# Windowed attention with a rational feed-forward network: transposes of q, k and P issued singly between the products of the network

## The chip, the core and the metric

The kernel runs on one core of a Trainium2 chip. A core has a matrix engine (TensorE, PE in the profile; its weight loads are shown apart as PEld), VectorE (DVE), ScalarE (ACT), GpSimd (POOL) and SyncE (SP), which here only issues DMAs. Each engine works through its own instructions in their order and waits on semaphores for the others. The metric is the device time of one execution in microseconds (us).

## The reference

Attention over a window, then a feed-forward network (FFN) whose activation is a ratio of polynomials. Cut to what matters:

```python
scores = q @ k.T / 8 + bias          # q, k, v: batch 4, heads 8, sequence 768, 64 each
scores = where(keep, scores, -1e9)   # keep: the last 96 keys, or one of the first 8
a = exp(scores - max); a = a / a.sum()
x = (a @ v) as [3072 tokens, 512]
h = x @ w_in                         # 512 -> 2048
P = a0 + a1*h + a2*h**2 + a3*h**3
Q = 1 + |b0|*|h| + |b1|*h**2
out = (P / (Q + 1e-6)) @ w_out       # 2048 -> 512
```

## The kernel before, in words

The 3072 tokens are cut into 12 chunks of 256 (TOK). A chunk has 8 attention units (two blocks of 128 queries, four pairs of heads) and 8 FFN units (two of the 16 tiles of 128 hidden features each). So there are 96 attention units u and 96 FFN units f. The function windowed() runs a pipeline over steps t: step t holds the splitting and transposing of q and k of unit t, the scores and the softmax of unit t-2, the transposing of its probabilities P for unit t-3, the product with v for two units at every odd step (st_pv), the first FFN product of f = t-12 (LAG) and the second of f-2 (F2).

Numbers are float32 held as a high and a low part in the type float32r, so each FFN product is taken three times (high by high, low by high, high by low). A step has on PE:

- st_ffn1: 24 products into a tile h, with 256 columns each (L258);
- st_ffn2: 12 products into two accumulators acc, with 512 columns each (L334); of each three, the third reads the low part of g, which POOL writes last (L314);
- st_score: 4 products into s (L408);
- st_qkT: 4 transposes of 128 x 128 into a tile tk (L378), from a tile sp that DVE and POOL write (L369, L370);
- st_pT: 4 transposes of P into a tile tp (L462), 2 in the first block of a sequence. From unit 30 (RAW) on P comes as float32r in the tile raw, which a DMA fills (L452) and which has one buffer; before unit 30 the transposes are plain float32;
- st_pv, at odd steps: 8 or 16 products into o, 64 output partitions each (L480).

The tiles tk, tp, s and o share three buffers in PSUM (pool ps_t). ACT copies tk out (L392, L395). DVE copies tp out (L465) from unit 21 (EARLY) on.

The order on each engine isn't that of the source. Each part gets a priority (base + 1000 t + a number from the table PRI), and the framework's scheduler walks a modelled timeline and issues, on each engine, what is ready by the model with the lowest priority first. That order is fixed when the program is built. In PRI, ffn1a is 150, qkT 200, pv 250, ffn1b 550, ffn2a 750, pT 800 and ffn2b 850: the four transposes of q and k stand between the two halves of st_ffn1, those of P between the two halves of st_ffn2, where they are ready by then.

Of the kernel before, what the change touches and what calls it, by code (L numbers as in the profile page):

```python
# [26 lines left out]
F2 = 2  # L27
# [68 lines left out]
def tile_kernel(ctx: ExitStack, tc: tile.TileContext, q, k, v, n_global, n_local,  # L96
# [11 lines left out]
    FPC = NFT // 2  # L108
    assert UPC == FPC == 8 and D == 64 and NT % 2 == 0
    NU = NCH * UPC  # L110
# [10 lines left out]
    def unit(u):  # L121
        c, j = divmod(u, UPC)
        t, p = divmod(j, NPAIR)
        b, i = divmod(2 * c + t, NT)
        return c, t, p, b, i

    def st_load(u):
        c, t, p, b, i = unit(u)
        hs = slice(2 * p, 2 * p + 4)
        r = slice(i * P, (i + 1) * P)  # L130
        n = pl.ldp.tile([P, 2, 4, D], F32, tag="nat", name=f"nat{u}")
        nc.sync.dma_start(out=n[:, 0], in_=q[b, hs, r, :].rearrange("h s d -> s h d"))
        nc.sync.dma_start(out=n[:, 1], in_=k[b, hs, r, :].rearrange("h s d -> s h d"))
        vt = pl.ldp.tile([P, 4, D], F32, tag="vt", name=f"vt{u}", bufs=6)
        nc.sync.dma_start(out=vt, in_=v[b, hs, r, :].rearrange("h s d -> s h d"))
        nat[u // 2] = n
        vts[u // 2] = vt
# [12 lines left out]
    def w_hi(key):  # L150
        if key[0]:
            return win_h[:, key[1], key[2] * 2 * TOK:(key[2] + 1) * 2 * TOK]
        return wout_h[:, key[1], :]

    def tmp(name):
        return pl.ffn.tile([P, 2, TOK], F32, tag="tmp", name=name, bufs=pl.tmps)
# [65 lines left out]
    a0, a1, a2, a3, b0, _, b1, q1 = (coef[:, x:x + 1] for x in range(8))  # L222
# [16 lines left out]
        nc.vector.tensor_scalar(out=k, in0=m, scalar1=0.0, scalar2=0.5, op0=ALU.is_gt, op1=ALU.mult)  # L239
        nc.vector.tensor_tensor(out=b1, in0=z, in1=k, op=ALU.mult)  # L240

    def st_ffn1(f, y):
        c, j = divmod(f, FPC)
        if y == 0:
            hps[f] = pl.ps_h.tile(sh, F32, tag="h", name=f"h{f}")
        jw, fw = divmod((2 * j + y) * P, 2 * TOK)
        fs = slice(fw, fw + P)
        if c == 0 and not pl.split:
            for ct in range(NCT):
                nc.tensor.matmul(out=hps[f][:, y, :], lhsT=full[1, ct, jw][:, fs], rhs=xT[c][:, ct, :],  # L250
                                 start=(ct == 0), stop=(ct == NCT - 1))
            return
        xh, xl = xT[c]
        n = 0
        for ct in range(NCT):
            wh, wl = w_hi((1, ct, jw)), low[1, ct, jw]
            for w, x in ((wh, xh), (wh, xl), (wl, xh)):
                nc.tensor.matmul(out=hps[f][:, y, :], lhsT=w[:, fs], rhs=x[:, ct, :],  # L258
                                 start=(n == 0), stop=(n == 3 * NCT - 1))
                n += 1  # L260

# [2 lines left out]
    def is_last(f):  # L266
        return f == NU - 1 and not pl.split
# [48 lines left out]
    def last_half(f, y):  # L316
        for st in (st_ew1, st_ew2, st_ew3, st_ew4):
            st(f, slice(y, y + 1))

    def st_ffn2(f, t):  # L320
        c, j = divmod(f, FPC)
        if j == 0:
            accs[c, t] = pl.ps_o.tile([P, DM], F32, tag="acc", name=f"acc{c}_{t}")
        acc = accs[c, t]
        ts = slice(t * P, (t + 1) * P)
        for y in range(2):
            ft = 2 * j + y
            if c == 0 and not pl.split:
                nc.tensor.matmul(out=acc, lhsT=gs[f][:, y, ts], rhs=full[0, ft],
                                 start=(ft == 0), stop=(ft == NFT - 1))  # L330
                continue
            wh = w_hi((0, ft))
            for n, (z, w) in enumerate(((0, wh), (0, low[0, ft]), (1, wh))):
                nc.tensor.matmul(out=acc, lhsT=gs[f][:, z, y, ts], rhs=w,  # L334
                                 start=(ft == 0 and n == 0), stop=(ft == NFT - 1 and n == 2))
        if j == FPC - 1:
            o = tmp(f"o{c}_{t}").rearrange("p a b -> p (a b)")
            rows = slice(c * TOK + t * P, c * TOK + (t + 1) * P)
            if is_last(f):
                (nc.vector.tensor_copy if t else nc.scalar.copy)(out=o, in_=acc)  # L340
            else:
                nc.any.tensor_copy(out=o, in_=acc)
            nc.sync.dma_start(out=out[rows, :], in_=o)
# [26 lines left out]
        nc.gpsimd.tensor_tensor(out=s[:, :, :, 1, :], in0=n, in1=s[:, :, :, 0, :], op=ALU.subtract)  # L370
        sp[u] = s

    def st_qkT(u):
        s = sp.pop(u)
        tk = pl.ps_t.tile([P, 2, 2, P], FR, tag="t", name=f"tk{u}")
        for z in range(2):
            for x in range(2):
                nc.tensor.transpose(out=tk[:, z, x, :], in_=s[:, z, x].rearrange("p a d -> p (a d)"),  # L378
                                    identity=ident_r)
        tqk[u] = tk  # L380


# [69 lines left out]
        nc.sync.dma_start(out=blocks_of(raw.bitcast(F32), i), in_=blocks_of(pr, i))  # L452
        prob[u] = (raw, None)

    def st_pT(u):
        i = unit(u)[4]
        pr, st = prob.pop(u)
        W = 2 if i else 1
        t_ps = pl.ps_t.tile([P, 2, 2, P], FR if u >= RAW else F32, tag="t", name=f"tp{u}")
        for x in range(2):  # L460
            for w in range(W):
                nc.tensor.transpose(out=t_ps[:, x, w, :], in_=pr[:, x, w, :], identity=ident_r if u >= RAW else ident)  # L462
        pT = pl.att.tile([P, 2, 2, P], F32, tag="pT", name=f"pT{u}", bufs=2)
        t_ps = t_ps.bitcast(F32) if u >= RAW else t_ps
        (nc.scalar.copy if u < EARLY else nc.vector.tensor_copy)(out=pT[:, :, 0:W, :], in_=t_ps[:, :, 0:W, :])  # L465
        pTs[u] = pT
# [33 lines left out]
        nc.vector.tensor_tensor(out=xl[:, p:p + 2, cs], in0=o_ps, in1=xh[:, p:p + 2, cs], op=ALU.subtract)  # L500


    ni = const.tile([P, 4], I32, name="ni")
    nf = const.tile([P, 4], F32, name="nf")

    def windowed():
        st_load(0)
        st_load(2)
        nc.sync.dma_start(out=ni[:, 0:2], in_=n_local.bitcast(I32).partition_broadcast(P))
        nc.sync.dma_start(out=ni[:, 2:4], in_=n_global.bitcast(I32).partition_broadcast(P))  # L510
        make_identity(nc, ident)
        nc.vector.tensor_copy(out=ident_r, in_=ident)
        nc.vector.tensor_copy(out=nf, in_=ni)
        load_coef()
        st_split(0)
        st_split(1)

        nl, ng = nf[:, 0:1], nf[:, 2:3]
        scr = tmp("scr").rearrange("p a (b w) -> p (a b) w", w=P)
        scr = [scr[:, x, :] for x in range(4)]  # L520
        window_masks(nc, scr, mask0, masks, nl, ng)

        base = tc.cur_priority
        for t in range(NU + LAG + F2):
            f = t - LAG
            pri = PRI_A if f < FPC else PRI

            def on(name, fn, u, *args):
                if 0 <= u < NU:
                    tc.cur_priority = base + 1000 * t + pri[name]  # L530
                    fn(u, *args)

            if t % 2 == 0:
                on("load", st_load, t + 4)
            on("score", st_score, t - 2)
            on("soft", st_soft, t - 2)
            on("ffn1a", st_ffn1, f, 0)
            on("qkT", st_qkT, t)
            if t % 2:
                on("pv", lambda u: st_pv(u // 2), t - 5)  # L540
            on("qkE", st_qkE, t)
            if t % 2:
                on("x", lambda u: st_x(u // 2), t - 5)
            if t:
                on("split", st_split, t + 1)
            if not is_last(f - 1):
                on("ew3", st_ew3, f - 1)
            on("norm", st_norm, t - 2)
            on("raw", st_raw, t - 2)
            if is_last(f):  # L550
                st_ew4(f - 1)
                last_half(f, 0)
                st_ffn1(f, 1)
                last_half(f, 1)
            else:
                on("ffn1b", st_ffn1, f, 1)
                on("ew1", st_ew1, f)
                if not is_last(f - 1):
                    on("ew4", st_ew4, f - 1)
                on("ew2", st_ew2, f)  # L560
            on("ffn2a", st_ffn2, f - F2, 0)
            on("pT", st_pT, t - 3)
            on("ffn2b", st_ffn2, f - F2, 1)
            for n, (kind, j) in enumerate(WSCHED.get(t, ())):
                tc.cur_priority = base + 1000 * t + pri["dec"] + 50 * n
                (load_win if kind else load_wout)(j)
            for n, key in enumerate(list(full)[SPLITS.get(f - 1, 0):SPLITS.get(f, 0)]):
                tc.cur_priority = base + 1000 * t + pri["wsplit"] + 4 * n
                split_w(key)
        tc.cur_priority = base + 1000 * (NU + LAG + F2 + 4)  # L570
# [154 lines left out]
```

## Time and profile before

| | |
|---|---|
| time, median of 3 runs | 794.26 us (793.93 to 798.46) |
| profiled execution: its time, its span | 792.2 us, 790.4 us |
| busy: PE, PEld | 743.9 us (94%), 649.6 us (82%) |
| busy: DVE, ACT, POOL | 599.6 us (76%), 575.1 us (73%), 533.3 us (67%) |
| granted clock of PE, mean | 0.992 |

A row of a timeline reads: start, duration, engine, line, operation, output and inputs, shape, count of instructions in the row, and in brackets the idle time before it and what ended it. Matmuls are pipelined, so a row's duration holds the time through the array as well; what one instruction costs in a stream is the distance from its start to the start of the next. The starts are printed in hundredths of a microsecond.

### The profile page before, as it was taken

To read this page: it belongs to the slowest core of one execution; us is meant where nothing else is said; L and a number is where in the kernel's file an instruction comes from. 1 tells how busy PE (TensorE), PEld (TensorE's weight loads), DVE (VectorE), ACT (ScalarE), POOL (GpSimd) and SP (SyncE) were. 2 spreads that over 40 slices of the span, in tenths; PEclk is the share of its full clock that TensorE was granted. 3 is DMA by queue.
4 is the path that set the end of the run, shared out by engine and by line. 5 is a ranking of instruction groups with operands and counts; after the bars stand their busy time and mean duration, and the time that the engine had idled before them with its cause. 6 is when DMAs were issued, how large, how long until landed. Compare 5 with 4: busy or idle time off the path is not lost.

```text
span 790.4 us, 15799 instructions
## 1 busy us (share of the span) xinstructions
PE 743.9 (94%) x5184; PEld 649.6 (82%) x5184; DVE 599.6 (76%) x1453; ACT 575.1 (73%) x1407; POOL 533.3 (67%) x572
## 2 busy tenths in 40 slices
PE   3688978899999999999999999999999999999995
PEld 2467647688998899999899999989999999988993
DVE  5889999987778676777776786777677786776664
ACT  4778677667887777777777777777877777766763
POOL 3868558979877667666667667666677777664440
PEclk9999999899999999999999999999999999999999
DMA  7785445212222233333332332333332332210000
GB/s 183 212 240 173 114 125 189 49 48 54 55 81 68 85 92 87 97 88 86 82 87 82 106 84 81 106 84 82 88 85 77 101 92 78 82 55 14 28 1 32
DMA packets 111932, 72.19 MB, mean 91 GB/s; under 512 B 82912, under 2 KB 97248, under 8 KB 111840
## 3 DMA queue, kind: packets, MB, share of 16 engines
q1 hardware_dynamic: 111840, 71.08, 32.0%
q8 instruction: 44, 0.72, 0.4%
q14 instruction: 48, 0.39, 0.2%
HBM read 35.92 MB, written 6.29 MB: 53 GB/s over the span
## 4 chain that ended last, share of the span: by engine, by line
PE 81%; DVE 6%; POOL 5%; DMA 4%; issue 2%; ACT 1%; SPq 0%; DVEq 0%; POOLq 0%; ACTq 0%
PE h L258 32%; PE acc L334 31%; PE o L480 5%; PE s L408 5%; PE tp L462 3%; PE tk L378 3%; DMA r<-in_moe_w_in_dram 2%; POOL pr L441 2%; PE h L250 1%; POOL sp L370 1%; DMA nat<-in_k_dram 1%; POOL fa L291 1%; DVE pr L419 1%; DVE fu L305 0%; DMA r<-in_moe_w_out_dram 0%
## 5 line engine op out<-in xcount | busy, mean ns | idle before, releaser
L334 PE MATMUL acc<-wout_h,g 128*128 128x512 f32 x704 | 242.8, 403 | 0.8 <-ACT g L313 0.8
L258 PE MATMUL h<-xh,win_h 128*128 128x256 f32 x704 | 205.4, 292 | 1.8 <-DVE fu L290 1.8
L441 POOL TENSOR_SCALAR pr<-pr,stats 128x256 f32<-128x256 f32 (+1 forms) x192 | 178.5, 940 | 39.2 <-issue 12.7
L258 PE MATMUL h<-xl,win_h 128*128 128x256 f32 x704 | 198.7, 282 | 0.0
L291 POOL TENSOR_TENSOR fa<-fa,fs 128x512 f32<-128x512 f32 x95 | 125.1, 1317 | 100.7 <-ACT fs L284 97.4
L334 PEld LDWEIGHTS acc<-wout_h,g 128*128 128x128 f32 x704 | 126.6, 188 | 21.8 <-ACT g L313 1.2
L258 PEld LDWEIGHTS h<-xh,win_h 128*128 128x128 f32 x704 | 133.3, 189 | 10.9 <-issue 6.2
L258 PEld LDWEIGHTS h<-xl,win_h 128*128 128x128 f32 x704 | 133.3, 189 | 2.3 <-issue 0.2
L429 ACT ACTIVATE pr<-pr,stats 128x256 f32<-128x256 f32 (+1 forms) x192 | 93.5, 492 | 53.5 <-DVE stats L419 53.4
L370 POOL TENSOR_TENSOR sp<-nat,sp 128x256 fp32r<-128x256 f32 x96 | 75.8, 790 | 73.5 <-DVE stats L432 41.0
L314 POOL TENSOR_TENSOR g<-fu,g 128x512 fp32r<-128x512 f32 x87 | 112.7, 1295 | 7.7 <-DVE fu L290 4.6
L282 ACT ACTIVATE fu<-h,coef 128x512 f32<-128x512 f32 (+1 forms) x97 | 75.4, 778 | 54.1 <-PE h L258 49.6
L303 DVE SCALAR_TENSOR_TENSOR fu<-fu,coef,q 128x512 f32<-128x512 f32 (+1 forms) x97 | 71.6, 738 | 36.2 <-ACT q L299 35.0
L298 ACT ACTIVATE fs<-fa,coef 128x512 f32<-128x512 f32 (+1 forms) x97 | 70.2, 724 | 30.3 <-POOL fa L291 27.9
L289 DVE TENSOR_TENSOR fu<-fu,h 128x512 f32<-128x512 f32 (+1 forms) x97 | 65.6, 677 | 16.9 <-ACT fs L284 14.9
L465 DVE COPY pT<-tp 128x512 f32<-128x512 f32 (+1 forms) x75 | 48.5, 646 | 35.7 <-PE tp L462 35.0
L369 DVE CAST sp<-nat 128x256 fp32r<-128x256 f32 x96 | 38.3, 399 | 46.7 <-PE tk L378 15.1
L290 DVE SCALAR_TENSOR_TENSOR fu<-fu,coef,h 128x512 f32<-128x512 f32 (+1 forms) x97 | 71.7, 739 | 2.5
L419 DVE CUSTOM_DVE_ANT_0 pr<-s,masks 128x256 f32<-128x256 f32 x160 | 61.4, 420 | 15.2 <-PE s L408 13.3
L408 PE MATMUL s<-kT,qT 128*128 128x256 f32 x384 | 70.5, 305 | 1.8 <-DMA qT<-qT 1.7
L304 DVE SCALAR_TENSOR_TENSOR q<-fa,coef,q 128x512 f32<-128x512 f32 (+1 forms) x97 | 72.1, 744 | 0.0
L408 PEld LDWEIGHTS s<-kT,qT 128*128 128x128 f32 x384 | 61.5, 203 | 9.0 <-DMA qT<-qT 1.9
(273 smaller groups left out, 1658.8 us busy)
## 6 DMA issues: line engine op xcount, KB each, us to landing
raw<-pr SPq DMA_DIRECT2D x58, 256.0 KB
qT<-qT SPq DMA_DIRECT2D x192, 64.0 KB
r<-in_moe_w_in_dram SPq DMA_DIRECT2D x16, 512.0 KB
r<-in_moe_w_out_dram SPq DMA_DIRECT2D x16, 512.0 KB
nat<-in_q_dram SPq DMA_DIRECT2D x48, 128.0 KB
nat<-in_k_dram SPq DMA_DIRECT2D x48, 128.0 KB
vt<-in_v_dram SPq DMA_DIRECT2D x48, 128.0 KB
out_dram<-o SPq DMA_DIRECT2D x24, 256.0 KB
```

Of the source, the lines that this page charges most:

```text
L258: nc.tensor.matmul(out=hps[f][:, y, :], lhsT=w[:, fs], rhs=x[:, ct, :], start=(n == 0), stop=(n == 3 * NCT - 1))
L282: nc.scalar.activation(out=u, in_=h, func=AF.Identity, scale=a3, bias=a2)
L290: nc.vector.scalar_tensor_tensor(out=u, in0=u, scalar=a1, in1=h, op0=ALU.add, op1=ALU.mult)
L291: side(f).tensor_tensor(out=a, in0=a, in1=s, op=ALU.add)
L303: nc.vector.scalar_tensor_tensor(out=u, in0=u, scalar=a0, in1=r, op0=ALU.add, op1=ALU.mult)
L304: nc.vector.scalar_tensor_tensor(out=r, in0=a, scalar=q1, in1=r, op0=ALU.add, op1=ALU.mult)
L314: side(f).tensor_tensor(out=g[:, 1, ys], in0=u, in1=g[:, 0, ys], op=ALU.subtract)
L334: nc.tensor.matmul(out=acc, lhsT=gs[f][:, z, y, ts], rhs=w, start=(ft == 0 and n == 0), stop=(ft == NFT - 1 and n == 2))
L370: nc.gpsimd.tensor_tensor(out=s[:, :, :, 1, :], in0=n, in1=s[:, :, :, 0, :], op=ALU.subtract)
L408: nc.tensor.matmul(out=s_ps[:, x], lhsT=qT[:, z, x, :], rhs=rhs, start=(z == 0), stop=(z == 1))
L429: nc.scalar.activation(out=d, in_=d, func=AF.Exp, scale=-1.0, bias=st[:, x:x + 1], accum_out=st[:, 2 + 2 * x:3 + 2 * x])
L441: nc.gpsimd.tensor_scalar(out=d, in0=d, scalar1=st[:, 6 + x:7 + x], scalar2=None, op0=ALU.mult)
```

## The change

st_ffn1, st_ffn2, st_qkT and st_pT become generators that pause after each instruction on PE. A new function weave runs two of them together: after every second product of the FFN it takes one transpose, with priorities that rise by 4 per product, so that the transposes have their places among the products of st_ffn1(f, 0) (12 products, q and k) and of both halves of st_ffn2 (12 products, P). It is used at steps 20 to 95 (FPC <= f < NU - 1 and t < NU); the other steps use the whole generators as before. What is computed is the same, and so is the number of instructions of each kind.

```diff
-    def st_ffn1(f, y):
+    def gen_ffn1(f, y):
...
                 nc.tensor.matmul(out=hps[f][:, y, :], lhsT=w[:, fs], rhs=x[:, ct, :],
                                  start=(n == 0), stop=(n == 3 * NCT - 1))
                 n += 1
+                yield
...
-    def st_ffn2(f, t):
+    def gen_ffn2(f, t):
...
                 nc.tensor.matmul(out=acc, lhsT=gs[f][:, z, y, ts], rhs=w,
                                  start=(ft == 0 and n == 0), stop=(ft == NFT - 1 and n == 2))
+                yield
...
-    def st_qkT(u):
+    def gen_qkT(u):
...
                 nc.tensor.transpose(out=tk[:, z, x, :], in_=s[:, z, x].rearrange("p a d -> p (a d)"),
                                     identity=ident_r)
+                yield
...
-    def st_pT(u):
+    def gen_pT(u):
...
                 nc.tensor.transpose(out=t_ps[:, x, w, :], in_=pr[:, x, w, :], identity=ident_r if u >= RAW else ident)
+                yield
...
+    def whole(gen):
+        def part(*args):
+            for _ in gen(*args):
+                pass
+        return part
+
+    st_ffn1, st_ffn2, st_qkT, st_pT = map(whole, (gen_ffn1, gen_ffn2, gen_qkT, gen_pT))
+
+    def weave(pri, main, other, every):
+
+        n = 0
+        for n, _ in enumerate(main):
+            if n % every == every - 1:
+                tc.cur_priority = pri + 4 * n + 2
+                next(other, None)
+            tc.cur_priority = pri + 4 * n + 4
+        for _ in other:
+            pass
...
-            on("ffn1a", st_ffn1, f, 0)
-            on("qkT", st_qkT, t)
+            woven = FPC <= f < NU - 1 and t < NU
+            if woven:
+                tc.cur_priority = base + 1000 * t + pri["ffn1a"]
+                weave(tc.cur_priority, gen_ffn1(f, 0), gen_qkT(t), 2)
+            else:
+                on("ffn1a", st_ffn1, f, 0)
+                on("qkT", st_qkT, t)
...
-            on("ffn2a", st_ffn2, f - F2, 0)
-            on("pT", st_pT, t - 3)
-            on("ffn2b", st_ffn2, f - F2, 1)
+            if woven and f - F2 >= 0:
+                tc.cur_priority = base + 1000 * t + pri["ffn2a"]
+                weave(tc.cur_priority, (x for y in range(2) for x in gen_ffn2(f - F2, y)), gen_pT(t - 3), 2)
+            else:
+                on("ffn2a", st_ffn2, f - F2, 0)
+                on("pT", st_pT, t - 3)
+                on("ffn2b", st_ffn2, f - F2, 1)
```

The order on PE around one group of transposes of q and k, before, at a step with products into o (a row ends with its count where it holds several instructions):

```order
L258 MATMUL h_8485<-xl_7291,win_h 128x256
L258 MATMUL h_8485<-xh_7290,w_3_2l 128x256
L378 MATMUL tk_8498<-ident_r,sp_8416 128x128 x4
L480 MATMUL o_8503<-pT_8366,vt_7555 64x128 x2
L480 MATMUL o_8503<-pT_8366,vt_7157 64x128 x2
L480 MATMUL o_8503<-pT_8464,vt_7555 64x128 x2
L480 MATMUL o_8503<-pT_8464,vt_7157 64x128 x2
L258 MATMUL h_8485<-xh_7290,win_h 128x256
```

The same step on PE now, at the transposes:

```order
L258 MATMUL h_8485<-xh_7290,win_h 128x256
L258 MATMUL h_8485<-xl_7291,win_h 128x256
L380 MATMUL tk_8488<-ident_r,sp_8416 128x128
L258 MATMUL h_8485<-xh_7290,w_0_2l 128x256
L258 MATMUL h_8485<-xh_7290,win_h 128x256
L380 MATMUL tk_8488<-ident_r,sp_8416 128x128
L258 MATMUL h_8485<-xl_7291,win_h 128x256
L258 MATMUL h_8485<-xh_7290,w_1_2l 128x256
L380 MATMUL tk_8488<-ident_r,sp_8416 128x128
L258 MATMUL h_8485<-xh_7290,win_h 128x256
L258 MATMUL h_8485<-xl_7291,win_h 128x256
L380 MATMUL tk_8488<-ident_r,sp_8416 128x128
```

And a little later in that step on PE, at the products into o:

```order
L258 MATMUL h_8485<-xl_7291,win_h 128x256
L258 MATMUL h_8485<-xh_7290,w_0_2l 128x256
L484 MATMUL o_8503<-pT_8370,vt_7555 64x128 x2
L484 MATMUL o_8503<-pT_8370,vt_7157 64x128 x2
L484 MATMUL o_8503<-pT_8468,vt_7555 64x128 x2
L484 MATMUL o_8503<-pT_8468,vt_7157 64x128 x2
L258 MATMUL h_8485<-xh_7290,win_h 128x256
```

One run of four has become four single transposes, each behind two products of the FFN, and the products into o, which followed the last transpose, now follow a product into h.

The transposes of P on PE, before:

```order
L334 MATMUL acc_0_8248<-wout_h,g_8349 128x512
L334 MATMUL acc_0_8248<-w_4l,g_8349 128x512
L334 MATMUL acc_1_8262<-wout_h,g_8349 128x512
L334 MATMUL acc_1_8262<-w_4l,g_8349 128x512
L258 MATMUL h_8485<-xh_7290,win_h 128x256
L258 MATMUL h_8485<-xl_7291,win_h 128x256
L258 MATMUL h_8485<-xh_7290,w_0_2l 128x256
L462 MATMUL tp_8459<-ident_r,raw_8326 128x128 x4
L334 MATMUL acc_0_8248<-wout_h,g_8349 128x512 x2
```

The same on PE now:

```order
L335 MATMUL acc_0_8248<-wout_h,g_8349 128x512
L335 MATMUL acc_0_8248<-w_4l,g_8349 128x512
L465 MATMUL tp_8455<-ident_r,raw_8326 128x128
L335 MATMUL acc_0_8248<-wout_h,g_8349 128x512 x2
L465 MATMUL tp_8455<-ident_r,raw_8326 128x128
L335 MATMUL acc_0_8248<-w_5l,g_8349 128x512
L335 MATMUL acc_0_8248<-wout_h,g_8349 128x512
L465 MATMUL tp_8455<-ident_r,raw_8326 128x128
L335 MATMUL acc_1_8262<-wout_h,g_8349 128x512
L335 MATMUL acc_1_8262<-w_4l,g_8349 128x512
L465 MATMUL tp_8455<-ident_r,raw_8326 128x128
```

Here too the run of four is taken apart, and the third product of an accumulator, the one that reads the low part of g, stands behind two products and one transpose, where four products, three of the next h and the transposes stood ahead of it.

## The prediction

> **What bounds the kernel now.** I read the page first: which engine is full, and what the chain of waits is made of.
>
> ```profile
> PE 743.9 (94%) x5184; PEld 649.6 (82%) x5184; DVE 599.6 (76%) x1453; ACT 575.1 (73%) x1407; POOL 533.3 (67%) x572
> PEclk9999999899999999999999999999999999999999
> PE 81%; DVE 6%; POOL 5%; DMA 4%; issue 2%; ACT 1%; SPq 0%; DVEq 0%; POOLq 0%; ACTq 0%
> ```
>
> PE carries 81% of the chain at a clock near full speed. An average over stages hides where it is full, so I cut the span into stretches with the view of windows (first column the length, then busy time and count by engine).
>
> ```profile
> 131.00:160.00 29.00, 25.23 (x143) 19.29 (x142) 28.26 (x63) 20.52 (x50) 27.10 (x24) 0.88 0.32 90
> 160.00:260.00 100.00, 100.00 (x722) 88.57 (x721) 79.31 (x181) 75.33 (x186) 79.30 (x83) 1.00 0.24 62
> 260.00:700.00 440.00, 440.00 (x3303) 398.66 (x3302) 322.88 (x807) 333.93 (x832) 307.27 (x341) 1.00 0.31 88
> 700.00:722.00 22.00, 22.00 (x158) 19.78 (x157) 16.88 (x36) 15.41 (x30) 11.26 (x10) 1.00 0.11 38
> ```
>
> From 160 to 722 us PE has no gap, while DVE has 440 - 322.9 = 117 us free in the long stretch, ACT 106 and POOL 133. Busy is not yet full, since a PE row also holds the time through the array, so I looked at whether starts follow each other at the pace of the work itself. The timeline of PE around one run of four transposes:
>
> ```profile
> 409.46 0.28 PE L258 MATMUL h<-xh,w_2l 128*128 128x256 f32 x1
> 409.58 0.46 PE L378 MATMUL tk<-ident_r,sp 128*128 128x128 f32 x4
> 409.87 0.35 PE L258 MATMUL h<-xh,win_h 128*128 128x256 f32 x1
> 410.06 0.28 PE L258 MATMUL h<-xl,win_h 128*128 128x256 f32 x1
> 410.18 0.29 PE L258 MATMUL h<-xh,w_2l 128*128 128x256 f32 x1
> 424.39 0.46 PE L378 MATMUL tk<-ident_r,sp 128*128 128x128 f32 x4
> ```
>
> A product into h starts 0.12 us after the one before it (410.06 to 410.18). The transposes of the next step but one begin at 424.39, 14.81 us on: a step takes 7.4 us. Its 24 products into h (2.8 us), 12 into acc (12 x 0.235 = 2.8, from the rows below) and 4 into s at the price of those into h (0.5), two groups of transposes (0.7) and half of a group into o make that up. So the pace is PE's own work, in order, and whatever the change adds to that work between 160 and 722 us is added to the time. All steps whose transposes are taken apart lie there.
>
> **What a transpose costs, alone and in a run.** The run of four at 409.58 delays the stream as follows: from its first start to the start of the second product behind it are 0.48 us, of which one product is 0.12, so four cost 0.36. The second product is the one to look at, since the first shows its start early and stays longer (0.35 instead of 0.28). The trace of before also has transposes of P in runs of one and three:
>
> ```profile
> 257.77 0.40 PE L334 MATMUL acc<-wout_h,g 128*128 128x512 f32 x1
> 258.01 0.40 PE L334 MATMUL acc<-w_10l,g 128*128 128x512 f32 x1
> 258.24 0.22 PE L462 MATMUL tp<-ident_r,raw 128*128 128x128 f32 x1
> 258.58 0.39 PE L334 MATMUL acc<-wout_h,g 128*128 128x512 f32 x1
> 259.27 0.37 PE L462 MATMUL tp<-ident_r,raw 128*128 128x128 f32 x3
> 259.48 0.46 PE L334 MATMUL acc<-wout_h,g 128*128 128x512 f32 x1
> 259.78 0.39 PE L334 MATMUL acc<-w_10l,g 128*128 128x512 f32 x1
> 265.07 0.22 PE L462 MATMUL tp<-ident_r,raw 128*128 128x128 f32 x1
> 265.42 0.39 PE L334 MATMUL acc<-wout_h,g 128*128 128x512 f32 x1
> 279.98 0.23 PE L462 MATMUL tp<-ident_r,raw 128*128 128x128 f32 x1
> 280.32 0.39 PE L334 MATMUL acc<-wout_h,g 128*128 128x512 f32 x1
> ```
>
> A product into acc takes 0.235 us (257.77, 258.01, 258.24). The three singles take 0.34, 0.35 and 0.34 to the second product behind them, less 0.235: 0.11 us each. The three in a run take 0.51 - 0.235 = 0.28. With 0.36 for four the costs are 0.11, 0.28, 0.36: about 0.084 for each transpose, and 0.027 more for each run, however long. Four singles cost 0.44 where a run costs 0.36.
>
> Why, the weight loads show:
>
> ```profile
> 258.01 0.14 PEld L462 LDWEIGHTS tp<-ident_r,raw 128*128 128x128 f32 x1
> 258.25 0.30 PEld L334 LDWEIGHTS acc<-wout_h,g 128*128 128x128 f32 x2
> 258.59 0.19 PEld L334 LDWEIGHTS acc<-w_11l,g 128*128 128x128 f32 x1
> ```
>
> The transpose's load, begun at 258.01, is hidden under the product before it. The product's load begins only with the transpose (258.25), and of the two merged loads the second begins at 258.25 + 0.30 - 0.19 = 258.36, 0.11 later: a product's load needs 0.11 us, and a single transpose, which streams 0.06 (its first in a run of four is followed that fast), can't cover it. In a run the next load is a transpose's, which is shorter. So a single hides one load and lays bare a longer one, four times over instead of once.
>
> The Trainium skill (TensorE: Matmul & The Clock Gate, section "LDWEIGHTS (loading the stationary operand)") prices any load at its columns over 1.2 GHz, an estimate of 107 ns for 128 columns. The single agrees; the run of four, at 0.36 and not 0.43, doesn't, and by that rule the taking apart would cost nothing and the whole change 2.0 us.
>
> **The change part by part.**
>
> 1. *Runs.* Counted in the order of the built programs, the float32r transposes (384 of q and k, 248 of P from unit 30 on) stand in 95 + 79 = 174 runs before and in 235 + 207 = 442 now; 369 of the runs now are single. Not every group is taken apart: at 19 steps those of q and k stand as three and one, at the early steps often still as four. 268 more runs x 0.027 = +7.2 us. Each of these numbers has an edge: at 0.020 for a run (singles of 0.105) it is 5.4, at 0.032 it is 8.6. No row shows a single between products into h; its load has the same 128 columns and type as that of acc, so I take the same price.
> 2. *Transposes of P in plain float32* (before unit 30): 46 runs before, 47 now. Nothing.
> 3. *What follows the transposes.* At odd steps the products into o stood behind the run and now stand behind a product into h. Both cases are in the trace:
>
> ```profile
> 253.51 0.28 PE L258 MATMUL h<-xh,w_3l 128*128 128x256 f32 x1
> 253.63 0.28 PE L258 MATMUL h<-xh,win_h 128*128 128x256 f32 x1
> 253.84 0.66 PE L480 MATMUL o<-pT,vt 128*64 128x128 f32 x8
> 402.04 0.46 PE L378 MATMUL tk<-ident_r,sp 128*128 128x128 f32 x4
> 402.42 0.66 PE L480 MATMUL o<-pT,vt 128*64 128x128 f32 x8
> ```
>
> A product into h ahead of o takes 0.21 instead of 0.12, 0.09 lost; a run of four ahead of o takes 0.38 instead of 0.36, 0.02 lost. The order has 41 such places behind transposes before and 12 now, 6 behind h before and 35 now: 29 x 0.07 = +2.0 us (between 0, if the o behind h hide it elsewhere, and 2.6).
>
> 4. *Moved earlier.* The first transpose of q and k comes up to ten products, 1.2 us, sooner. Its operand is long there, as in the step shown above:
>
> ```profile
> 403.06 0.74 POOL L370 TENSOR_TENSOR sp<-nat,sp 128x256 fp32r<-128x256 f32 x1
> ```
>
> It ends at 403.80, 5.8 us ahead of 409.58: free. The transposes of P read raw, whose DMA waits for the last transpose of the unit before, as there is one buffer:
>
> ```profile
> 378.50 0.64 SPq L452 DMA_DIRECT2D raw<-pr  x1
> 383.55 0.29 PE L462 MATMUL tp<-ident_r,raw 128*128 128x128 f32 x2
> ```
>
> Here 5.05 us from issue to use suffice without a gap on PE. Now the last of P stands 6 products and 3 transposes behind the first, 6 x 0.235 + 3 x 0.11 = 1.74 us, so 7.4 - 1.7 = 5.7 us remain from the last to the next unit's first, less the few tenths to the issue. Enough, as far as these rows tell. Behind the DMA on SP's queue stand the loads of later units and the moves of qT; they are used a step or more later.
> 5. *Moved later.* DVE's copy of P (L465) now waits for a last transpose that is 1.5 us further from the first than in a run (1.74 against 0.21). On DVE's queue behind it stand the next polynomial step (L290) and the reading of the scores; DVE's 117 us free over 440 / 7.4 = 60 steps are 1.96 us a step, so 1.5 fit. What is late next is g:
>
> ```profile
> 483.20 1.29 POOL L314 TENSOR_TENSOR g<-fu,g 128x512 fp32r<-128x512 f32 x1
> 485.54 0.40 PE L334 MATMUL acc<-wout_h,g 128*128 128x512 f32 x1
> ```
>
> The tightest step I found has 485.54 - 484.49 = 1.05 us between g and the first product into acc, and the third product, the first that reads that part, now comes 2 x 0.235 + 0.11 = 0.58 later: 1.6 us of cover against 1.5 of delay. I cost it at nothing.
>
> Sum: 7.2 + 2.0 = +9.2 us. The profiled execution (792.2, its span 790.4 and 1.8 around it) would take 801.4; the median of the runs, 794.26, lies 2.1 higher, so 803.5.
>
> **The rivals.**
>
> *Faster: the loads are hidden.* If PE fetched the load behind a single early, under the product ahead, a single would cost only its 0.06 us. Per row: 369 singles x 0.06 = 22.1, the other 263 transposes in 73 runs 263 x 0.084 + 73 x 0.027 = 24.1, together 46.2, against 632 x 0.084 + 174 x 0.027 = 57.8 before: -11.6, with the 2.0 of o -9.6, and 784.7 us. It decides at a single of about 0.086. For it speaks that loads do run under products; against it, that all three singles shown take 0.11. The Trainium skill (same page, section "Part 2: What happens when you issue a matmul") says that PE pulls loads ahead of running matmuls into a background buffer. The trace agrees for one load ahead and shows none for two. Chance 0.07.
>
> *No change that can be measured.* If a transpose costs the same in a run as alone (0.11 by the load behind it, which is what the skill's rule on loads above comes to), or the added pace is given back where other engines were late, only the o remain: about 796.3. For it speaks that the run's advantage rests on differences of hundredths; against it, that runs of one, three and four fit one line, and that PE has no gap to give back in. Chance 0.13.
>
> *Slower still: g or the copy of P becomes late.* The mechanism of 5: where the copy's delay exceeds the 1.6 us of cover, PE stands in order at the third product. Each 0.1 us beyond it, over the 63 steps with raw, is 6.3 us: 809.8 for 0.1. Against it speak the waits of DVE, 28.2 us in that stretch for P already, which PE never feels. Chance 0.10.
>
> ```profile
> DVE pT L465 <- PE tp L462: 28.2, 36, 1.7
> ```
>
> **How the numbers follow.** What this kernel's measurement can tell from no change is about 1%, 8 us: below 786.3 is faster, above 802.2 slower. The forecast (0.70) is 803.5, with 5.4 + 0 and 8.6 + 2.6 as the bounds of its terms 799.7 to 805.5; a quarter of it, 0.18, falls below 802.2. Faster 0.07; same 0.13 + 0.18 = 0.31; slower 0.52 + 0.10 = 0.62. The range goes from 796, the second rival, to 810, the third, and leaves out the first and parts of these two.
>
> **What would show it.** In the profile after: PE still without a gap from 160 to 722 us and the stretch some 9 us longer; singles at 0.11 between products into h too; steps of 7.5 instead of 7.4 us; no wait of PE for POOL's g or for raw. Singles at 0.06 would prove the first rival, unchanged steps the second; a wait of PE for g or for raw, or a stretch ahead of 160 us of another length, would make the number wrong for a reason that isn't in the sum.

## The result, and the profile after

The change takes 803.1 us in the median of its runs (798.74 to 805.61), the kernel before 794.1 us: a ratio of 1.0112, with a 95% interval of 1.0088 to 1.0136. Slower, by 9.0 us: little, but clear of the noise. The profiled execution is the lowest of the six, 798.74 us with a span of 796.9; experiments 7 and 9 to 11 look at why the totals differ.

The windows of the kernel after, with the same columns as before:

```profile
131.00:160.00 29.00, 26.52 (x167) 20.41 (x166) 27.98 (x63) 21.84 (x54) 27.10 (x25) 0.93 0.29 77
160.00:260.00 100.00, 99.42 (x716) 88.48 (x715) 82.71 (x187) 75.73 (x189) 79.28 (x83) 1.00 0.25 64
260.00:700.00 440.00, 440.00 (x3232) 391.10 (x3231) 309.33 (x787) 328.18 (x815) 298.82 (x335) 1.00 0.30 86
```

PE is still without a gap in the long stretch, but where 3303 of its instructions began there, 3232 do now: 2% fewer. Almost nothing new holds it up, since its waits from 160 to 715 us are one row, a single wait that lies ahead of 260 us:

```profile
PE h L258 <- DVE fu L291: 0.6, 1, 0.6
```

So the time went into the stream itself. The timeline of PE at transposes of q and k that stand singly, and, behind the dots, at products into o:

```profile
274.02 0.28 PE L258 MATMUL h<-xl,win_h 128*128 128x256 f32 x1
274.13 0.22 PE L380 MATMUL tk<-ident_r,sp 128*128 128x128 f32 x1
274.19 0.33 PE L258 MATMUL h<-xh,w_1l 128*128 128x256 f32 x1
274.36 0.28 PE L258 MATMUL h<-xh,win_h 128*128 128x256 f32 x1
274.48 0.23 PE L380 MATMUL tk<-ident_r,sp 128*128 128x128 f32 x1
274.55 0.33 PE L258 MATMUL h<-xl,win_h 128*128 128x256 f32 x1
274.71 0.28 PE L258 MATMUL h<-xh,w_1l 128*128 128x256 f32 x1
274.83 0.22 PE L380 MATMUL tk<-ident_r,sp 128*128 128x128 f32 x1
275.07 0.28 PE L258 MATMUL h<-xl,win_h 128*128 128x256 f32 x1
...
282.60 0.28 PE L258 MATMUL h<-xh,w_1l 128*128 128x256 f32 x1
282.81 0.77 PE L484 MATMUL o<-pT,vt 128*64 128x128 f32 x10
```

Each single takes 0.23 or 0.24 us to the second product behind it (274.13 to 274.36, 274.48 to 274.71, 274.83 to 275.07), less 0.12 for a product: 0.11, as between products into acc. The first product behind a transpose stays 0.33 instead of 0.28, which is the time its load is late. And the product ahead of o takes 0.21.

To measure this apart from everything else I take one **stretch** in every kernel: from the first product into acc of FFN unit 24 to that of unit 81, 57 steps. Between these two marks each of the kernels compared here issues the same instructions on PE (684 products into acc, 1368 into h, 228 into s, 432 into o, 440 transposes). The marks in the timeline, before:

```profile
279.50 0.40 PE L334 MATMUL acc<-wout_h,g 128*128 128x512 f32 x1
699.67 0.39 PE L334 MATMUL acc<-wout_h,g 128*128 128x512 f32 x1
```

and after:

```profile
277.19 0.39 PE L335 MATMUL acc<-wout_h,g 128*128 128x512 f32 x1
706.03 0.41 PE L335 MATMUL acc<-wout_h,g 128*128 128x512 f32 x1
```

420.17 us before, 428.84 after: +8.67, or 0.152 us a step. In this profile the part ahead of the stretch is 2.3 us shorter, and that is why its total is only 6.5 us above the first profile of before.

### The profile page after: what moved, and what is told of

Same layout as the page of the kernel before. It is cut to its first block, busy times and chain, and to the rows that moved or that the text cites. A ratio compares the mean times of both kernels' runs of the same rounds, so it can differ in the third digit from the quotient of the medians.

```text
span 796.9 us, 15820 instructions
## 1 busy us (share of the span) xinstructions
PE 749.5 (94%) x5184; PEld 646.9 (81%) x5184; DVE 595.2 (75%) x1453; ACT 574.3 (72%) x1407; POOL 532.1 (67%) x572
## 4 chain that ended last, share of the span: by engine, by line
PE 79%; DVE 8%; POOL 5%; DMA 3%; issue 2%; ACT 1%; SPq 0%; DVEq 0%; POOLq 0%; ACTq 0%
PE h L258 33%; PE acc L335 31%; PE o L484 5%; PE s L411 5%; PE tp L465 3%; PE tk L380 3%; POOL pr L444 2%; DMA r<-in_moe_w_in_dram 1%; POOL sp L372 1%; DMA nat<-in_k_dram 1%; DVE pr L422 1%; POOL fa L292 1%; DVE fu L291 1%; DVE fu L290 1%; DVE fu L306 1%
## 5 line engine op out<-in xcount | busy, mean ns | idle before, releaser
L335 PE MATMUL acc<-wout_h,g 128*128 128x512 f32 x704 | 246.3, 407 | 0.8 <-ACT g L314 0.8
L335 PEld LDWEIGHTS acc<-wout_h,g 128*128 128x128 f32 x704 | 122.7, 189 | 25.9 <-ACT g L314 1.2
L315 POOL TENSOR_TENSOR g<-fu,g 128x512 fp32r<-128x512 f32 x87 | 112.7, 1295 | 11.7 <-ACT g L314 7.0
L290 DVE TENSOR_TENSOR fu<-fu,h 128x512 f32<-128x512 f32 (+1 forms) x97 | 65.8, 679 | 66.9 <-ACT fs L285 59.2
L380 PE MATMUL tk<-ident_r,sp 128*128 128x128 f32 x384 | 67.7, 242 | 15.6 <-POOL sp L372 13.7
L285 ACT ACTIVATE fs<-h,coef 128x512 f32<-128x512 f32 (+1 forms) x97 | 66.5, 685 | 0.2
```

The source lines that it names most:

```text
L290: nc.vector.tensor_tensor(out=u, in0=u, in1=h, op=ALU.mult)
L315: side(f).tensor_tensor(out=g[:, 1, ys], in0=u, in1=g[:, 0, ys], op=ALU.subtract)
L335: nc.tensor.matmul(out=acc, lhsT=gs[f][:, z, y, ts], rhs=w, start=(ft == 0 and n == 0), stop=(ft == NFT - 1 and n == 2))
```

## The experiments

Two theories stood against each other: that each run of float32r transposes costs 0.027 us beside 0.084 for each transpose, with 0.07 for each group of products into o that stands behind h instead of a transpose; or that the new places and the shuffled order of the other engines cost the time. The counts in the expectations are those of the whole program; those of the stretch are taken from the traces. The medians, each beside that of the kernel before on the same chip, also hold what lies outside the stretch.

### 1. The same places, the runs left whole

```diff
-            if n % every == every - 1:
+            if n == 7:
                 tc.cur_priority = pri + 4 * n + 2
-                next(other, None)
+                for _ in other:
+                    pass
```

> The woven kernel, but each group of four transposes is issued whole at one place, after the eighth product. The framework's scheduler still parts some: 216 runs of float32r transposes in its order (174 before, 442 in the change), 33 products into o behind h (6 before). Theory (each run costs 0.027 us more, each o behind h 0.07): 42 x 0.027 + 27 x 0.07 = +3.0 us on before, 797.1. Rival (the new places and the shuffled order on the other engines cost the time, not the taking apart): as the change, about 803.

The median is 797.64 us against 792.87 for the kernel before, a ratio of 1.0054 (1.0035 to 1.0073). The marks:

```profile
279.57 0.39 PE L335 MATMUL acc<-wout_h,g 128*128 128x512 f32 x1
702.75 0.40 PE L335 MATMUL acc<-wout_h,g 128*128 128x512 f32 x1
```

The stretch is 423.18 us, +3.0. The scheduler still parts many groups into pairs: in the stretch stand 163 runs where before has 123, and 28 groups of o behind h or acc where it has none: 40 x 0.027 + 28 x 0.07 = 3.0. The rival falls: new places and a new order, with most runs of four whole, give a third of the change's loss in the stretch, and that third is accounted for. (The median is 4.8 us up; the 1.8 us beyond the stretch aren't accounted for.)

### 2. Pairs in place of singles

```diff
-            if n % every == every - 1:
+            if n % 4 == 3:
                 tc.cur_priority = pri + 4 * n + 2
                 next(other, None)
+                next(other, None)
```

> The woven kernel with two transposes after every fourth product in place of one after every second: 235 runs, 33 o behind h. Theory: 61 x 0.027 + 27 x 0.07 = +3.5 us, 797.6; runs of two at 0.195 us each. Rival (places and order): about 803. A second rival (the load behind a run is laid bare only where a run is a single): the same total, but runs of two at 0.17.

The median is 796.48 us, a ratio of 1.0039 (1.0016 to 1.0062). Marks:

```profile
282.74 0.39 PE L335 MATMUL acc<-wout_h,g 128*128 128x512 f32 x1
705.86 0.40 PE L335 MATMUL acc<-wout_h,g 128*128 128x512 f32 x1
```

The stretch is 423.12, +2.95, with 183 runs and 27 o behind h or acc: 60 x 0.027 + 27 x 0.07 = 3.5 expected. The runs of two with a product into h ahead and two behind cost 0.194 us in the median of 58, so the second rival falls too: the load behind a run is laid bare behind a pair as behind a single.

### 3 and 4. One kind of transposes woven, the other not

Only q and k, and then only P:

```diff
-            if woven and f - F2 >= 0:
+            if False:
```

```diff
-            if woven:
+            if False:
```

> Only the transposes of q and k are woven; those of P stand as before. 324 runs, 35 o behind h. Theory: 150 x 0.027 + 29 x 0.07 = +6.1 us, 800.2. Rival (most of the cost comes with P, whose copy and DMA stand behind a later last transpose): within 2 us of before.

> Only the transposes of P are woven; those of q and k stand in runs of four. 287 runs, 28 o behind h. Theory: 113 x 0.027 + 22 x 0.07 = +4.6 us, 798.7. Rival (the cost comes with P): about 802 or more.

With q and k alone the median is 800.81 us, a ratio of 1.0077 (1.0047 to 1.0108); with P alone 801.65, 1.0098 (1.0065 to 1.0131), from four runs. The marks of the first:

```profile
281.08 0.40 PE L335 MATMUL acc<-wout_h,g 128*128 128x512 f32 x1
707.44 0.39 PE L335 MATMUL acc<-wout_h,g 128*128 128x512 f32 x1
```

and of the second:

```profile
281.99 0.39 PE L335 MATMUL acc<-wout_h,g 128*128 128x512 f32 x1
706.29 0.40 PE L335 MATMUL acc<-wout_h,g 128*128 128x512 f32 x1
```

426.36 us and 424.30: +6.2 and +4.1, where 145 x 0.027 + 29 x 0.07 = 5.9 and 106 x 0.027 + 21 x 0.07 = 4.3 were to be expected. Both rivals, by which the cost comes with P, fall: q and k alone cost the stretch 6.2 us. The two don't add up to the change, since either alone already moves most of the products into o behind h. The total of the second run, 8.8 us above before, is near what its rival named and well over the 4.1 of its stretch, so it was taken again (11).

All together, for the stretch:

| kernel | runs | o behind h or acc | worked out | measured |
|---|---|---|---|---|
| before | 123 | 0 | | 420.17 |
| runs whole (1) | 163 | 28 | +3.0 | +3.0 |
| pairs (2) | 183 | 27 | +3.5 | +2.95 |
| P alone (4) | 229 | 21 | +4.3 | +4.1 |
| q and k alone (3) | 268 | 29 | +5.9 | +6.2 |
| the change | 379 | 29 | +8.9 | +8.7 |

### 5 and 6. Transposes that cover the load behind them

If a single costs more because of the load of the product behind it, and not because the stream is broken, a slower transpose must cost the same in a run and alone. In plain float32 transposes are slower: in a run they start 0.11 us apart, as long as the load of a product needs. Both kernels keep all transposes of P in float32; the second also weaves them (with the edit of experiment 4):

```diff
-RAW = 30
+RAW = 96
```

> The kernel before with all transposes of P in plain float32 (RAW = 96), in its own order: 133 runs of them. Base for the next run. Theory: a float32 transpose streams about 0.11 us, so that it covers the load of the product behind it, and costs 0.11 alone or in a run: from unit 30 on 248 x 0.11 in place of 248 x 0.084 + 79 x 0.027, +4 us on before, about 797.

> The run before this one (all transposes of P in float32) with the transposes of P woven as in the change, those of q and k in runs of four: 248 runs of P instead of 133, 28 o behind h instead of 6. Theory (a single costs more only where it streams shorter than the load behind it): nothing for the runs, 22 x 0.07 = +1.5 us on the float32 base, and singles at 0.11 as in runs. Rival (every break of the stream of products costs 0.027 whatever the type): 115 x 0.027 + 1.5 = +4.6 us on that base.

Medians: 800.06 us (1.0064 of before, 1.0042 to 1.0086) and 800.98 (1.0085, 1.0069 to 1.0100). A run of four float32 transposes in the first:

```profile
285.02 0.60 PE L462 MATMUL tp<-ident,pr 128*128 128x128 f32 x4
285.38 0.48 PE L334 MATMUL acc<-wout_h,g 128*128 128x512 f32 x1
285.69 0.39 PE L334 MATMUL acc<-w_0l,g 128*128 128x512 f32 x1
```

and singles in the second:

```profile
282.63 0.27 PE L465 MATMUL tp<-ident,pr 128*128 128x128 f32 x1
282.66 0.47 PE L335 MATMUL acc<-w_1l,g 128*128 128x512 f32 x1
282.97 0.39 PE L335 MATMUL acc<-wout_h,g 128*128 128x512 f32 x1
283.20 0.27 PE L465 MATMUL tp<-ident,pr 128*128 128x128 f32 x1
283.23 0.48 PE L335 MATMUL acc<-wout_h,g 128*128 128x512 f32 x1
283.54 0.39 PE L335 MATMUL acc<-w_0l,g 128*128 128x512 f32 x1
```

Four in a run take 0.67 - 0.235 = 0.435 us, a single 0.34 - 0.235 = 0.105: no price for the taking apart. The weight loads show why. Before, at the run of float32r transposes at 409.58 (the first of these rows holds the last three loads of the run):

```profile
409.58 0.31 PEld L378 LDWEIGHTS tk<-ident_r,sp 128*128 128x128 f32 x3
409.84 0.19 PEld L258 LDWEIGHTS h<-xh,win_h 128*128 128x128 f32 x1
409.94 0.19 PEld L258 LDWEIGHTS h<-xl,win_h 128*128 128x128 f32 x1
```

and in the float32 base, at the run shown above:

```profile
285.02 0.36 PEld L462 LDWEIGHTS tp<-ident,pr 128*128 128x128 f32 x3
285.35 0.19 PEld L334 LDWEIGHTS acc<-wout_h,g 128*128 128x128 f32 x1
285.46 0.19 PEld L334 LDWEIGHTS acc<-w_0l,g 128*128 128x128 f32 x1
```

Three float32r loads take 0.26 us until the product's load begins, three float32 ones 0.33. Over the whole stretch the next load begins 0.085 us after that of a float32r transpose in a run (medians 0.085 and 0.086), 0.108 after that of a float32 one, and 0.108 after that of a product behind a transpose, be it alone or the last of a run. So a transpose is paced by the load of what stands behind it: in a run of float32r that is a short load, except behind the last, and 0.108 - 0.085 = 0.023 is nearly the whole price of 0.027. In float32 the two loads are equal and there is no price. Whether a float32 transpose also streams as long as that load, these rows don't tell.

The marks of the two:

```profile
283.61 0.40 PE L334 MATMUL acc<-wout_h,g 128*128 128x512 f32 x1
707.85 0.40 PE L334 MATMUL acc<-wout_h,g 128*128 128x512 f32 x1
```

```profile
281.61 0.39 PE L335 MATMUL acc<-wout_h,g 128*128 128x512 f32 x1
706.47 0.40 PE L335 MATMUL acc<-wout_h,g 128*128 128x512 f32 x1
```

424.24 and 424.86. The float32 base is 4.1 us above the stretch of before, near the 4 worked out for the whole program (its total, 5.9 above, carries more). Weaving P costs 0.6 us here where it costs 4.1 in float32r. The rival (every break of the stream costs 0.027) wanted over 4. The 21 groups of o behind h should have cost 1.5 alone; why only 0.6 appears is not settled; part of it is that the float32 singles came out a shade under a quarter of a run.

### 7, 9, 10 and 11. Where the totals vary

The change, the kernel before (twice) and P alone, run once more without a new edit.

> The change once more, for its second profile: the stretch from the 8-times-24th FFN unit's second product to the 81st's is 428.85 us in the first profile. Theory (the pace of PE's own work): 428.9 within 0.3 again, whatever the total, and the spread of the totals (798.7 to 805.6) lies ahead of that stretch. Rival (the spread comes from waits inside the stretch): the stretch differs by as much as the totals.

> The kernel before once more, for a second profile and a comparison with itself. Theory: the stretch from the first product into acc of FFN unit 24 to that of unit 81 takes 420.2 us again, within 0.3; what lies ahead of it (279.50 us in the first profile) differs by one to three us from run to run, in this kernel as in the change (277.19 and 281.51). Rival: the part ahead is steady in this kernel (279.5 within 0.3), and only the changed orders make it vary.

> A third profile of the kernel before, as the run ahead of it: 420.2 us for the stretch, and the part ahead somewhere between 277 and 283.

> Only the transposes of P woven, once more, since its four runs came out 8.8 us above before where the stretch was 4.1 us longer. Theory: the stretch is 424.3 us again, and the total settles between 4 and 7 us above before, with what lies ahead of the stretch carrying the rest. Rival (a cost in the part ahead that belongs to this order): again 8 us or more above before, with a part ahead of 282 us or more in its profile.

(The marks are those defined above; the first of these expectations means by "second product" the product into acc, of FFN units 24 and 81.) The change took 803.57 us (1.0121 of before, 1.0106 to 1.0137); before against itself 794.13 (1.0001, 0.9983 to 1.0020) and 794.06 in a single run; P alone 797.78 (1.0046, 1.0025 to 1.0066). The marks of the change in its second profile, and of before in its second:

```profile
281.51 0.39 PE L335 MATMUL acc<-wout_h,g 128*128 128x512 f32 x1
710.36 0.41 PE L335 MATMUL acc<-wout_h,g 128*128 128x512 f32 x1
```

```profile
281.38 0.40 PE L334 MATMUL acc<-wout_h,g 128*128 128x512 f32 x1
701.55 0.39 PE L334 MATMUL acc<-wout_h,g 128*128 128x512 f32 x1
```

428.85 again, 420.17 again, and in the third profile of before (281.02 to 701.19) 420.17 once more; P alone (281.72 to 706.02) 424.30 again. The stretch repeats to a hundredth of a microsecond, so the waits that the rival of the first expectation puts there don't exist. What varies lies ahead of it, in the kernel before too, against the rival of the second. There the granted clock of PE, which is 1.00 from 160 to 700 us in all of these profiles, falls to half in short pieces of 3.4 or 6.8 us, and not equally often:

| profile | mean granted clock, 0 to 160 us | time at half clock on record there | first mark |
|---|---|---|---|
| before | 0.97 | 10.2 us | 279.50 |
| before, second | 0.96 | 13.7 us | 281.38 |
| before, third | 0.96 | 13.7 us | 281.02 |
| the change | 0.98 | 6.8 us | 277.19 |
| the change, second | 0.96 | 13.7 us | 281.51 |
| P alone | 0.97 | 10.2 us | 281.99 |
| P alone, second | 0.95 | 17.1 us | 281.72 |

In the first two kernels more time at half clock goes with a later mark, by half of that time or a little more. So the 2.3 us that the first profile of the change seemed to win there are no effect of the order: its second profile has the mark where before has its own. P alone doesn't follow the clock, so that this isn't the whole of the spread.

P alone, 8.8 us above before at first, came out at 3.3 the second time, below the 4 to 7 that were expected. The rival of 8 us and more falls with it. Its two profiled executions took nearly the same time (799.52 and 799.23 us); where its other runs differ no profile shows.

### 8. Fewer runs than before

If runs cost, fewer should gain. From step 33 on, the transposes of P and of q and k are issued in one run behind the eleventh product into acc, and the products into o behind them:

```diff
+                def both():
+                    yield from gen_pT(t - 3)
+                    yield from gen_qkT(t)
+                    if t % 2:
+                        st_pv((t - 5) // 2)
+                    yield
+                    st_qkE(t)
+                    if t % 2:
+                        st_x((t - 5) // 2)
...
-            if n % every == every - 1:
+            if n == 10:
                 tc.cur_priority = pri + 4 * n + 2
-                next(other, None)
+                for _ in other:
+                    pass
```

> The opposite edit: from step 33 on the transposes of P and of q and k stand together in runs of eight, behind the eleventh product of the second FFN product, and the products into o behind them. 120 runs of float32r transposes instead of 174 in the kernel before, 43 o behind a transpose of q and k, 9 behind acc (4 before). Theory: -54 x 0.027 + 5 x 0.08 = -1.1 us on before, and 1.1 us less in the stretch of 57 steps (419.1 where before has 420.17). Rival (x comes later in its step, and the first FFN product of a chunk waits for it): slower by some tenths at each of 11 chunks.

It took 810.96 us, 1.0231 of before (1.0207 to 1.0254): the slowest of all, where 1.1 us less than before was forecast. The scheduler left 77 runs in the stretch, 33 of them of eight. A run of eight itself does what the line says:

```profile
297.50 0.46 PE L465 MATMUL tp<-ident_r,raw 128*128 128x128 f32 x4
297.80 0.50 PE L380 MATMUL tk<-ident_r,sp 128*128 128x128 f32 x4
298.14 0.35 PE L258 MATMUL h<-xh,w_2l 128*128 128x256 f32 x1
298.33 0.28 PE L258 MATMUL h<-xh,win_h 128*128 128x256 f32 x1
```

0.83 - 0.12 = 0.71 us, where the line gives 0.70 and two runs of four take 0.73. (By the Trainium skill, TensorE: Matmul & The Clock Gate, section "LDWEIGHTS (loading the stationary operand)", eight loads of 107 ns would be an estimate of 0.86; the trace doesn't agree.) But PE is no longer without a gap, as the row of the window from 260 to 700 us shows (429.78 us busy of 440). The two largest rows of its waits from 279 to 715 us stand below it:

```profile
260.00:700.00 440.00, 429.78 (x3162) 384.08 (x3161) 310.08 (x769) 317.33 (x789) 291.61 (x326) 0.99 0.30 84
PE acc L335 <- POOL g L315: 8.0, 5, 2.4
PE tp L465 <- DMA raw<-pr: 1.1, 3, 0.6
```

Of the 16.8 us lost, 10.2 are waits from 279 to 715 us, and 8.0 of these are waits for g, the cover that the other orders leave and this one doesn't; the rival named in the expectation (x late at the chunks) is not what the waits show. A further part is the granted clock, 0.99 from 260 to 700 us and 1.00 there in the profile of before: behind the two longest waits (1.9 us to 466.9 and 2.4 us to 593.0) the trace has it at half for 3.4 us each, an estimate of 3.4 us lost. The stretch, in which this order holds 15 products into h and 16 into o fewer, is 435.11 us. The rest, some 3 us and the gain that was forecast, stays open. No version that beats the kernel before came out of this.

## Why the prediction was right

- *The bound.* PE without a gap from 160 to 722 us but for 0.6, so that what is added to its work is added to the time: the stretch grew by 8.7 us and the medians by 9.0, against a forecast of 9.2 (803.5, measured 803.1). That the total agrees to 0.4 us is in part luck, as totals repeat less well than that; the test is the stretch, where the same sum with the stretch's counts gives 8.9.
- *Runs, +7.2 us.* The line of 0.027 for a run and 0.084 for a transpose was read from runs of one, three and four in the trace of before. It holds for pairs (0.194) and for eight (0.71), for singles between products into h, which no row had shown, and through five changed orders to 0.6 us of a stretch of over 420. That the longer load of the product is the cause, and not the break as such, is shown by the loads, 0.108 us for a product and 0.085 for a float32r transpose in a run, and by the float32 transposes, whose loads are as long as the product's and which cost the same in runs and alone. The picture of the prediction holds with one sharpening: a run hides no load behind the transposes either, it lays bare shorter ones.
- *o behind h, +2.0 us.* 0.21 for the product ahead of o, as read from a single place, is also the median of the 29 places of the stretch after; in the table the term carries most of what experiments 1 and 2 lose. In experiment 6 it came out smaller than worked out, and that is open. Why a product loses time there is not shown, only that it does.
- *P in float32, nothing.* In experiment 6 singles and runs cost the same.
- *Moved earlier, nothing.* From 160 us on PE waited neither for sp nor for raw in the change. In experiment 8 it did wait for raw (1.1 us), so that this cover was real and not large.
- *Moved later, nothing.* Right in the sum, wrong in its picture. The copy of P was to wait 1.5 us longer on DVE; its waits fell instead, from 28.2 us to 11.7 (260 to 700 us):

```profile
DVE pT L469 <- PE tp L465: 11.7, 13, 1.5
```

  In the new order a step of the polynomial (L289 before, L290 now) stands ahead of the copy on DVE, where it stood behind it, and takes up part of the time in which the last transpose was waited for. The third rival, g late, didn't come about in the change; experiment 8 shows it in another order, with 8.0 us of waits.
- *The first rival* (loads hidden two ahead) is refuted by the singles in the trace after: behind a single the load of the next product takes its 0.108 us in the median, between products into acc as between those into h, where this rival needed a single of 0.06. *The second* (no change) was the nearest: the measured 1.1% is just past the 1% that I took as the limit, and its interval begins at 0.9%.
- *What the prediction didn't have* is the spread of the part ahead of the stretch. I named a different length there as a sign of a reason outside the sum; it turned out to differ between profiles of one and the same kernel, by 1.9 us before and 4.3 in the change, largely along with the time at half clock.

## What to carry to other kernels

Where PE is full, ask of each short matmul not what it costs but whether it takes as long as the load of the next one: one that doesn't lays that load bare. If the loads of its like are shorter than those of the long products, as for the float32r transposes here, it belongs in a run with its like and not between long products; if they are equal, as in float32, a run gains nothing. Such prices are in the trace already, wherever the scheduler has happened to part a run; three or four places give the line, and counts from the order do the rest. And measure a change of this size over a stretch with equal instructions on both sides, since the total carries the spread of the start with it.

## What the runs showed of the hardware that was not expected

- The same program repeats 57 steps to 0.01 us (420.17 three times, 428.84 and 428.85, 424.30 twice), while the part ahead of them, where PE isn't full and its clock falls to half in pieces of 3.4 or 6.8 us, varies by up to 4.3 us in one kernel (277.19 and 281.51).
- A product into h or acc ahead of the narrow products into o (64 output partitions) loses 0.09 us (0.21 for 0.12), four times what a transpose loses there (0.02). Whether the change of shape is the reason was not tested.
- In a run the load of a float32r transpose takes 0.085 us and that of a plain float32 transpose 0.108, like that of a product in float32r, all of 128 x 128.
- A plain float32 transpose of 128 columns costs 0.11 us alone and in runs, a float32r one 0.11 alone and 0.09 in a run of four (0.36): the faster type keeps its gain only in runs.
